# Block means of the first batch's values: ten products in one group of 32 array columns, or in four groups in turn with one product that adds them

## The chip, the cores and the metric

One NeuronCore of a Trainium2 chip. The time is device microseconds of one execution of the program. TensorE (PE) multiplies, VectorE (DVE), ScalarE (ACT) and GpSimd (POOL) do the element-wise work, SyncE (SP) requests the DMA transfers.

## What is computed

Two batches of windowed attention with block summaries, whose output goes through two feed-forward networks; the second network has the same shape, with another activation:

```python
B, H, S, D = 2, 8, 768, 64
block, window = (32, 16)
k_sum = k.reshape(B, H, nb, block, D).max(axis=3)
v_sum = v.reshape(B, H, nb, block, D).mean(axis=3)
# scores over a window of +-16 positions and over the 24 block maxima, one softmax over both
scores_all = np.concatenate([scores_l_m, scores_s], axis=-1)
v_all = np.concatenate([v, v_sum], axis=2)
x = np.matmul(a, v_all)                  # then 1536 tokens x 512
h = x @ w_in                             # 512 x 2048
out = activation(h) @ w_out              # 2048 x 512
```

The change is in `v_sum` of the first batch.

## The kernel before

Tokens are worked in 12 groups of 128 (six to a batch). A group g goes through `scores(g)` (PE products into two PSUM banks, then on DVE mask, scale and minimum, L520), `softmax(g)` (exponentials on ACT, L534, and the shares), `turn(g)` (transposes on PE, L574, and copies to SBUF), and `values(g)` (products on PE, L591, then a rounded copy, L601, and the rest, L603, into the two halves of the network's input). One chunk of the network is 512 tokens, so groups 0 to 3 must be through `values` before the first `first_product` (L637) can start. From there on products of the networks and the groups 4 to 11 alternate on PE.

Weights arrive as 64-bit numbers; `convert` and `split` (L298 to L327) turn each half of a weight tile into two single-precision parts by six passes on POOL, ACT and DVE.

`v_sums0` makes the 24 block means of the first batch. Six passes t run over the 768 positions. For t < 4 two products read the windowed values tiles (96 rows each, `blkw_sb`), for t = 4 and 5 one product reads 128 rows loaded for this alone (`v_a`, `blk_sb`). All ten accumulate in partitions 96 to 127 of one bank, `hs[3]`. The means are then copied to rows 96 to 119 of the six values tiles (L445 from PSUM for two of them, L449 from the first tile for the others), because `values` reads them as extra rows of its operand. `v_sums1` does the same for the second batch with 128-column products in four groups of the array's columns (L471).

Nothing is left to a scheduler. Every piece of work is an operation added with `Plan.add`, which takes the data it reads and writes and, where several engines could do it, their forms. `PICK` holds one digit for each such operation, the form taken. `ORDER` holds two characters for each operation, its number; the operations of each engine are issued in this order, and `Plan.idle` puts filler products of zeros (L1045) where it expects PE to wait. DMA requests all go through SP's queue in the same order. The tile framework adds the waits.

```python
                if t < 4:
                    for w in range(2):
                        mm(ps[96:P, :], blkw_sb[:, w, t, :], v[:96, w, :], start=(t + w == 0), stop=False)
                else:
                    mm(ps[96:P, :], blk_sb[:, t, :], v_a[:, t - 4, :], start=False, stop=(t == NG - 1))
```

Of the kernel before, what the change touches and what calls it, by code (L numbers as in the profile page):

```python
# [14 lines left out]
ALU = mybir.AluOpType  # L15
AX = mybir.AxisListType
# [5 lines left out]
NB = S // BLK  # L22
P = 128
# [28 lines left out]
    '0000230000000000001100111010000000011100001100000000000001000000110000000101110000001010000000000010'  # L52
    '0000000000000001000000000011020000002000001000100002001000200010000000000010000120010000001201001101'
    '0100100000110100010011010001001101011000201110001100101010111110000000101000001000001000000000000200'
    '1100000000011100000000100000010100002110001011001100001100010100000100110000010111100110100111000111'
    '1011000101000110100101010010100011011101010000111100010010110110011010111010101001010101011001011110'
    '1111110101011011000010111101100100010100011111000100110010001011000000110101011011100100111101001001'
    '01101000001111111000111101010011000101'
)
ORDER = (  # L60
    "###(#4#)#;#$#2#6#0#8#%%>#9#:#5#&%E#3#<#'#7#W#1%Z#V$&%?#?#B$(%@$7$'$.%A%F$8#=$)#@$9#A%L%H$Y%G$*$/%B$0"
    "$?%I#+$+$,&%$-$:$H$@$1$A&#$2%J$3$;&$$B%K$<$5$4$C&7$=%C$I#F#C$6$>%S$J$K#D&&#>$F#E$D&'$P%M#G$E%D$Z%N%#"
    "#H%$&0&)%O$L$Q&8$R%P#*#,$M&U&9#I&:%T'#%)$N%%&;#-%&%V$O&<#J$S%*%Q%'#K&=%+%U$T#.'H$G%($U#L#N$W$V#X#O%,"
    "#Z%W%.%-#P$#%2$X#Y#Q&3&Y&*#R%0&V&W%5&1%3&,#S%/%4%8%1'$%R%6%;%9%7%X#/'I':%<%:%Y(Y&+%=#T&2&-&>'J'K&4$%"
    "&.*X'L&5&/&?'M$$&@&D&(&Z&A&I'N&E&X+.+$&F(,&J&G&K&B'%&H*Y';&L&C')#M&M+%&N&6&P+/&O&Q+&*Z+2'<&R+0'.+#'*"
    "+<&S+3(-+''/(/+1(.&T#U+('B+4'&'++=+)'0+5',+*'-+J+@'1''+6'2'((H++'5+A+>'3+7'6+?+,'=+B(M(I+-,$+C'V'>+8"
    "'D+K(%+D+9'O'4+E+L'7+F+N+M(N+:+X+O'8(O,#+G(J+Q+;+Y'W,%'A+R+Z(P'Y,&'?'X,4'@'9'C+H(&,5(Z'Z,('P)#,2+I('"
    ")8'E(#(K+P(L(Q,3'G($'Q,E'F),(T(:,G(():(0(R(U+S,D(S'R,F)'+T(V'S+U(1,6()+V)()-,'(*).+W))(W'T(;)*)/,),X"
    "(2,:(X,Y(<(=)0)$,+,*)+(>'U,H)%,,)&,7(+(3)>,;,-,8(A)1)3(?,V)2)4(@,L,W,<)C)5)?,.,/,Z,9)6,I)@)D(6)E,0)7"
    ",J,=,M,K)A,>);,N)F,?,1,O-4)<)Q-#)O-&,@1Z)B)G)9)=(B-',P-1,A(C-2-(-5-$)J-8)P(D-3(4-%1L-0(5,Q)H,B-F-9)I"  # L70
    ',C)K-:-),R)Z(E(7-B-*,S)L-J-+-E,T*#-,-G-C,U)M(8-X-K)U-6)N--*$*%-7-D(9-Y)R.$)V-L)W1S-H-..%1M-;-U)X1O-I'
    "(F)S-W-<-T2%1N(G)T.6-M*&)Y2)-=*.-N*0-/*9-V->-O*'.1-?*(*).7-P...:-Q.0***:.&*/*;*4./-Z1P*+.8.;-R.H.#*<"
    ".<-@*,-A.'*-*5.22*1V*1.31T.(.4*6.L.Z*=*21U*3*G-S.).I*@*7.F/#.**8.5.X.+/&.E.9*L/'.D.M*>.J.W2#.=.V.K.>"
# [12 lines left out]
    "808S:%8V8R:18J918.;,8W928H848I8C:28L948X8K8E8M858D8Y868N958O96:'9)9+97939*9,8Z:-989/9-:P9#:390999.:Q"
    '9$;L:4;/:5;-9%9:;N9&9;9C9A:69<9@9E;2:7:&9B:.:9;M;P;0:(;&:W:/9F;1:)9D9=;3;R;.::9?;6;4;T9>;59G;O;79J;S'
    ";'9K;Q9I:;<#9H:X;Y;8;><$;9;E;U9N:8;V;:9O9V<%9L;;<&9M9Y>2;W9S;<9Z9P;=9T<;;Z9W;X>9</9X<69Q<5<'9R;?<=<<"
    '<(;@<)<A<><*:#<?>:>3<99U<B>4<4<@<+<C>5>;<0<,<8><<->6=B<1;F<J<E<2<D<.<V=C;A>7<W>=>8>@<F>>>?<:<G>A<H>B'
    ">C=T<I>D<K>E<L<N>V<M<R<3<O>F<7<S<P>G=U=D<Q?%<T=E<U;B=V?B=L=W;G=M<X?F>W?&;C?C;D?D?';H>H>X<Y;I>&=$?(=%"  # L90
    "?E<Z>Y;J=#;K?J?)=F>O>Z=)?#?*=(>'='=,=&?+?H?$=N>K=-?,=+=*?M?I?-?K?.=.>I?/?G=1>J?0=/?2=2?1?L=0B(?3=4B/"
    '=8=6?OB+B)?N=5?P=9B0=G===O>P@1B2=<@2?Q=:=@B*=3B,=7?R=;@3=?>(=>=X@7?U=Y=A@4@9>)@8@%@5@;B1?Y>LA8>QB3?V'
    "@:>R?ZA9B-@#@6B.@&>S=KB4B6=SB5=JB7=RB8=IB9B<B:@<=H@==PB;>M@>B=?SBL@'?T=Z@?>N>%>*@$?4=Q>.BS>$?W>#@@?X"
    '>T>-@AAKBMBO?5BN@(@B>U>1>+@L?;@H>,@M@D@,@C>/?7@)BT?6@IAJ@E?<BVBP>0@*BQ?8@.BU@F@+A:@0A;@/?9@-@G?:C8@N'
    'AB@O?=@RAC@J@SBW@K@PC9@QAL?>ATC:??BXA<?@C@?AA=C;BEB>BR@U@TAUBZCC@XBY@WBF@VC>@ZAMA$C#A#C<C$C(C)A&C?A*'
    "@YA(BHA'C%C=F%A+C&CGD'C'ADCHA%EVD(A)BAA,F&B?A-CACEEWD/CFEXAEA.EYCBA1A/A3D)D-D*EZA0F(D.A2D1E.AVA7BGAW"
    "CDANA5B@A6F'AABBCKD+A4CSAOBICOAICTA?CLCUA@D0CVAGF)AHAQA>AFBCCIF#BDE/BJBKF$C*D,C1CPAYF,F*D4CQCMCJARF+"
# [98 lines left out]
def tile_kernel(ctx, tc, qT, kT, kw, vw, vt, w1, w2, av, bv, masks, ident, blk, out):  # L199
# [220 lines left out]
    def v_sums0():  # L420
# [17 lines left out]
        for t in range(4, NG):  # L438
            load_v(t)
# [677 lines left out]
```

## Time and profile before

| | us |
|---|---|
| median of three runs | 589.99 |
| lowest and highest | 589.51, 591.37 |
| span of the profiled execution (first to last instruction) | 587.4 |
| PE busy in it | 578.6 |
| DVE, ACT, POOL busy | 494.4, 348.5, 294.7 |

The span is one execution under the profiler; the run's time is 2.6 us more at the median, which is what lies around the span. The granted clock of TensorE is 1.00 of full speed in every window of the profile. A product of single-precision operands stands in the trace as two records, each with its weight load. Times in the rows below are from the span's start.

### The profile page before, as it was taken

To read this page: it belongs to the slowest core of one execution; us is meant where nothing else is said; L and a number is where in the kernel's file an instruction comes from. 1 tells how busy PE (TensorE), PEld (TensorE's weight loads), DVE (VectorE), ACT (ScalarE), POOL (GpSimd) and SP (SyncE) were. 2 spreads that over 40 slices of the span, in tenths; PEclk is the share of its full clock that TensorE was granted. 3 is DMA by queue.
4 is the path that set the end of the run, shared out by engine and by line. 5 is a ranking of instruction groups with operands and counts; after the bars stand their busy time and mean duration, and the time that the engine had idled before them with its cause. 6 is when DMAs were issued, how large, how long until landed. Compare 5 with 4: busy or idle time off the path is not lost.

```text
span 587.4 us, 9645 instructions
## 1 busy us (share of the span) xinstructions
PE 578.6 (98%) x3608; PEld 466.6 (79%) x3613; DVE 494.4 (84%) x887; ACT 348.5 (59%) x648; POOL 294.7 (50%) x272
## 2 busy tenths in 40 slices
PE   8999999999999999999999999999999999999997
PEld 4477788888888888888888888888888888888886
DVE  5999999999989898988899998968687786866643
ACT  3988998988676677658657455524540434424410
POOL 1777676573475657654766472131423175523210
PEclk9999999999999999999999999999999999999999
DMA  8986534301222223110000141320313023002005
GB/s 311 352 306 209 192 118 151 104 30 35 73 71 73 76 101 110 37 36 2 17 20 1 37 143 37 107 73 0 144 32 113 1 73 126 18 0 73 1 1 214
DMA packets 17983, 53.10 MB, mean 90 GB/s; under 512 B 2273, under 2 KB 2785, under 8 KB 17937
## 3 DMA queue, kind: packets, MB, share of 16 engines
q1 hardware_dynamic: 17936, 52.49, 26.1%
q8 instruction: 28, 0.46, 0.3%
q14 instruction: 19, 0.15, 0.1%
HBM read 48.55 MB, written 3.15 MB: 88 GB/s over the span
## 4 chain that ended last, share of the span: by engine, by line
PE 94%; DMA 2%; DVE 1%; SPq 1%; issue 1%; POOL 0%; ACT 0%; DVEq 0%
PE y L654 23%; PE y L850 22%; PE hb L637 15%; PE hc L812 13%; PE hs L637 8%; PE hc L939 7%; PE hs L591 2%; PE hs L507 2%; PE hs L574 1%; DMA mask_sb<-in_masks 1%; DMA k<-in_blk 1%; SPq L280 1%; DVE s L520 0%; POOL s L549 0%; PE hs L434 0%
## 5 line engine op out<-in xcount | busy, mean ns | idle before, releaser
L654 PE MATMUL y<-g,wt 128*128 128x512 f32 x576 | 139.1, 392 | 0.0
L654 PEld LDWEIGHTS y<-g,wt 128*128 128x128 f32 x576 | 106.8, 188 | 22.3 <-POOL g L745 0.3
L850 PE MATMUL y<-wt,g 128*128 128x512 f32 x480 | 116.1, 389 | 0.0
L850 PEld LDWEIGHTS y<-wt,g 128*128 128x128 f32 x480 | 90.1, 188 | 18.7
L637 PE MATMUL hb<-xx,wt 128*128 128x512 f32 x384 | 89.5, 389 | 0.0
L325 POOL TENSOR_TENSOR wt<-raw,wt 128x512 fp32r<-128x512 f32 x44 | 62.4, 1425 | 51.0 <-DVE wt L322 30.4
L637 PEld LDWEIGHTS hb<-xx,wt 128*128 128x128 f32 x384 | 72.1, 188 | 15.0
L309 ACT ACTIVATE raw<-raw 128x512 f32<-128x512 f32 x62 | 41.1, 676 | 33.3 <-POOL raw L305 24.6
L717 POOL TENSOR_TENSOR q<-q,u 128x512 f32<-128x512 f32 x34 | 46.2, 1368 | 23.8 <-ACT u L707 14.4
L828 POOL TENSOR_TENSOR g<-t,g 128x512 fp32r<-128x512 f32 x17 | 23.4, 1380 | 63.3 <-ACT g L825 63.3
L825 ACT ACTIVATE g<-t 128x512 fp32r<-128x512 f32 x40 | 25.0, 628 | 49.4 <-PE y L850 43.4
L305 POOL TENSOR_SCALAR raw<-raw 128x512 f32<-128x512 f32 x44 | 35.8, 815 | 34.1 <-DMA raw<-in_w 33.9
L286 ACT ACTIVATE wt<-raw 128x512 fp32r<-128x512 f32 x56 | 36.8, 671 | 25.7 <-POOL raw L796 6.6
L313 DVE SCALAR_TENSOR_TENSOR raw<-raw 128x512 int32<-128x512 int32 x62 | 47.7, 779 | 4.3 <-ACT raw L309 4.1
L637 PE MATMUL hs<-xx,wt 128*128 128x512 f32 x192 | 47.8, 398 | 0.0
L812 PE MATMUL hc<-wt,wt 128*128 128x512 f32 x192 | 47.4, 389 | 0.0
L745 POOL TENSOR_TENSOR g<-t,g 128x512 fp32r<-128x512 f32 x22 | 30.6, 1397 | 30.3 <-ACT g L739 25.8
L939 PE MATMUL hc<-xx,wt 128*128 128x512 f32 x192 | 45.6, 389 | 0.0
L865 DVE SCALAR_TENSOR_TENSOR part<-y,part 128x512 f32<-128x512 f32 x36 | 24.4, 684 | 22.1 <-PE y L850 22.0
L939 PEld LDWEIGHTS hc<-xx,wt 128*128 128x128 f32 x192 | 36.0, 188 | 7.5
L812 PEld LDWEIGHTS hc<-wt,wt 128*128 128x128 f32 x192 | 36.0, 188 | 7.5
L637 PEld LDWEIGHTS hs<-xx,wt 128*128 128x128 f32 x192 | 35.1, 188 | 7.7 <-issue 0.2
(175 smaller groups left out, 1097.6 us busy)
## 6 DMA issues: line engine op xcount, KB each, us to landing
raw<-in_w SPq DMA_DIRECT2D x62, 512.0 KB, 4.2
vv<-in_vw SPq DMA_DIRECT2D x6, 512.0 KB, 7.1
out<-part SPq DMA_DIRECT2D x12, 256.0 KB, 2.9
k<-in_kT SPq DMA_DIRECT2D x4, 384.0 KB, 3.7
q<-in_qT SPq DMA_DIRECT2D x6, 256.0 KB, 7.5
e<-in_kT SPq DMA_DIRECT2D x4, 384.0 KB
raw<-in_vt SPq DMA_DIRECT2D x3, 512.0 KB, 5.1
e<-in_vw SPq DMA_DIRECT2D x3, 512.0 KB
```

What stands on the lines that cost most here:

```text
L286: nc.scalar.activation(out_, in_, AF.Copy)
L305: eng.tensor_scalar(out=hif, in0=hif, scalar1=CAP, scalar2=-CAP, op0=ALU.min, op1=ALU.max)
L309: add(ACT, 0.58, lambda: nc.scalar.activation(hif, hif, AF.Prelu, scale=REBIAS, alpha=2.0 ** 32), [kr], [(kr, 1)])
L313: add(DVE, 0.61, lambda: nc.vector.scalar_tensor_tensor(out=lo, in0=hi, scalar=3, in1=lo, op0=ALU.logical_shift_left, op1=ALU.bitwise_or), ...
L325: eng.tensor_tensor(out=to()[:, 1], in0=src, in1=to()[:, 0], op=ALU.subtract)
L637: mm(ps, lt, rt, start=(k == 0), stop=(k == 11))
L654: mm(y, lt, rt, start=(i == 0 and j == 0), stop=(i == HALF - 1 and j == 2))
L717: eng.tensor_tensor(out=q2[a][:, w], in0=q2[a][:, w], in1=u2[:, w], op=ALU.mult)
L745: eng.tensor_tensor(out=g2[a][:, 1, w], in0=t2[a][:, w], in1=g2[a][:, 0, w], op=ALU.subtract)
L812: mm(bank_at(bank_), left(lp, kk), right(rp, kk), start=(j == 0), stop=(j == 5))
L850: mm(yb[d], lt, rt, start=(j == 0 and e == 0), stop=(j == QUART - 1 and e == 2))
L939: mm(bank_at(2 * a + u), w_at(n)[:, lp, kk * P:(kk + 1) * P], x_of(2)[:, rp, kk, :], start=(j == 0), stop=(j == 11))
```

## The change

The ten products no longer all go to partitions 96 to 127. Product w of pass t < 4 goes to group c = (2t + w) mod 4 of 32 columns (partitions 32c to 32c + 31), passes 4 and 5 to groups 0 and 1; the first product in each group starts its sum, the last one ends it. Then the whole bank is copied to SBUF (`part`, on ACT or DVE by the form) and one product with `four_sb`, four 32x32 identities one below the other, adds the four groups into partitions 96 to 127, from where all goes on as before. `four_sb` is made on DVE from the identity matrix. The warm-up products become one operation instead of four. `PICK` and `ORDER` are new as a whole; the order of issue differs in all parts of the kernel.

```diff
+    four_sb = k_0[:, 3808:3840]
...
-        for n in range(4):
-            add(PE, 1.5, lambda: [mm(hs[2], z[:, :P], z, start=True, stop=True) for _ in range(4)],
-                ["z"], [("h", 2)])
+        add(PE, 6.0, lambda: [mm(hs[2], z[:, :P], z, start=True, stop=True) for _ in range(16)], ["z"], [("h", 2)])
...
+        add(DVE, 0.2, lambda: nc.vector.tensor_reduce(
+            out=four_sb, in_=id_sb.rearrange("p (x m) -> p m x", m=32), op=ALU.add, axis=AX.X), ["id"], ["four"])
...
-                if t < 4:
-                    for w in range(2):
-                        mm(ps[96:P, :], blkw_sb[:, w, t, :], v[:96, w, :], start=(t + w == 0), stop=False)
-                else:
-                    mm(ps[96:P, :], blk_sb[:, t, :], v_a[:, t - 4, :], start=False, stop=(t == NG - 1))
-
-            add(PE, 1.72 if t < 4 else 0.86, go, [("v", "b"), vk] if t < 4 else ["blk", ("v", "a", t - 4)], [("h", 3)],
+
+                parts = [(blkw_sb[:, w, t, :], v[:96, w, :]) for w in range(2)] if t < 4 else [(blk_sb[:, t, :], v_a[:, t - 4, :])]
+                for w, (mean, rows) in enumerate(parts):
+                    c = (2 * t + w) % 4 if t < 4 else t - 4
+                    mm(ps[32 * c:32 * c + 32, :], mean, rows, start=(t < 2), stop=(t >= 3))
+
+            add(PE, 0.9 if t < 5 else 0.5, go, [("v", "b"), vk] if t < 4 else ["blk", ("v", "a", t - 4)], [("h", 3)],
                 fresh=(("h", 3),) if t == 0 else ())
+        part, pk = vs, [("vs", c) for c in range(4)]
+        add(ACT, 0.5, lambda: nc.scalar.copy(part, ps), [("h", 3)], pk,
+            more=[(DVE, 0.6, lambda: nc.vector.tensor_copy(part, ps), False)])
+        add(PE, 0.9, lambda: mm(ps[96:P, :], four_sb, part, start=True, stop=True), ["four", *pk], [("h", 3)])
...
-            old = [("k", 0, p) for p in range(4)] + [("q", "b"), "blk"]
+            old = [("k", 0, p) for p in range(4)] + [("q", "b"), "blk", "four"]
```

How the new order of issue stands on PE until the first product, read from the two strings:

| before | after |
|---|---|
| scores 0, 1, 3, 2 | scores 0, 1, one turn of 0, scores 3, 2 |
| both turns of 0, means t = 0, both turns of 1 | means t = 0, a turn of 1, the other of 0, means t = 1, 2, the other turn of 1 |
| means t = 1, 2, 3, 4, 5 | means t = 3, 4, 5, the product with `four_sb` |
| turns of 2, a turn of 3, values 0, the other turn of 3 | turns of 2, values 0, a turn of 3, values 1, the other turn of 3 |
| values 1, 2, 3, scores 4, first product | values 2, 3, scores 4, first product |

The last diff line lets chunk 2 of the network's input, which takes over the tile in which `four_sb` stands, wait for its reader.

## Rows read from the trace of the kernel before

**Rows 1.** Page, part 1: busy us (share of the span) and instructions of each engine.

```profile
PE 578.6 (98%) x3608; PEld 466.6 (79%) x3613; DVE 494.4 (84%) x887; ACT 348.5 (59%) x648; POOL 294.7 (50%) x272
```

**Rows 2.** Windows: length, busy us (instructions) by engine, PEclk, DMA share, GB/s.

```profile
...
10.00:20.00 10.00, 8.40 (x229) 6.06 (x225) 9.26 (x55) 9.17 (x31) 6.29 (x10) 1.00 1.04 395
20.00:30.00 10.00, 9.68 (x31) 2.96 (x29) 9.57 (x39) 9.68 (x36) 7.49 (x14) 1.00 0.98 333
30.00:40.00 10.00, 8.68 (x212) 6.88 (x211) 9.87 (x18) 8.73 (x17) 7.46 (x8) 1.00 0.98 319
40.00:60.00 20.00, 19.58 (x277) 15.75 (x274) 18.53 (x72) 17.99 (x58) 16.53 (x18) 1.00 0.60 207
60.00:80.00 20.00, 19.91 (x211) 15.72 (x201) 19.55 (x51) 19.19 (x47) 12.42 (x14) 1.00 0.56 182
80.00:100.00 20.00, 20.00 (x239) 16.31 (x238) 18.99 (x58) 18.07 (x47) 15.34 (x15) 1.00 0.42 137
...
```

**Rows 3.** PE timeline: start, us, instruction, count, [idle before <-releaser].

```profile
19.22 1.90 PE L432 MATMUL hs<-vv,e 96*32 96x512 f32 x4 [0.24 <-DMA vv<-in_vw]
...
22.07 5.34 PE L432 MATMUL hs<-vv,e 96*32 96x512 f32 x12
...
27.73 1.88 PE L434 MATMUL hs<-v_a,k 128*32 128x512 f32 x4 [0.32 <-DMA k<-in_blk]
...
31.62 1.15 PE L591 MATMUL hs<-pt,vv 120*64 120x64 f32 x32
...
36.46 1.03 PE L1045 MATMUL hs<-z 128*128 128x512 bf16 x4 [0.16 <-issue]
...
38.72 0.40 PE L507 MATMUL hs<-k,q 64*64 64x96 f32 x8
...
39.97 3.01 PE L637 MATMUL hs<-xx,wt 128*128 128x512 f32 x12
```

**Rows 4.** DVE and ACT timelines, from the mask to the last values copies.

```profile
10.62 0.28 DVE L520 CUSTOM_DVE_ANT_0 s<-y,mask_sb 128x120 f32<-128x120 f32 x1 [1.51 <-DMA mask_sb<-in_masks]
...
36.71 1.27 DVE L603 TENSOR_TENSOR xx<-hs,xx 128x512 fp32r<-128x512 f32 x2
...
11.32 0.38 ACT L534 ACTIVATE s<-s,stat 128x120 f32<-128x120 f32 x1
...
36.61 0.57 ACT L601 CAST xx<-hs 128x512 fp32r<-128x512 f32 x1
```

**Rows 5.** Request queue's timeline, page part 6 (last: us to landing), chain of waits.

```profile
30.40 0.44 SPq L280 DMA_DIRECT2D q<-in_qT  x1
...
q<-in_qT SPq DMA_DIRECT2D x6, 256.0 KB, 7.5
...
21.45 6.15 DMA k<-in_blk
```

**Rows 6.** PE timeline: the second batch's block means, in four column groups.

```profile
58.72 1.52 PE L471 MATMUL hs<-raw,k 128*32 128x128 f32 x48 [0.24 <-ACT pt L577]
```

**Rows 7.** Groups by line and shape, 8 to 40 us: busy, mean ns.

```profile
L313 DVE SCALAR_TENSOR_TENSOR raw<-raw 128x512 int32<-128x512 int32 x7 | 4.6, 681 | 0.0
...
L325 DVE TENSOR_TENSOR wt<-raw,wt 128x512 fp32r<-128x512 f32 x2 | 1.9, 940 | 0.0
...
L376 DVE TENSOR_REDUCE ks<-e 128x24 f32<-128x768 f32 x2 | 1.9, 938 | 0.0
...
L578 DVE COPY t<-hs 120x512 f32<-120x512 f32 x2 | 1.4, 688 | 0.1
...
L305 DVE TENSOR_SCALAR raw<-raw 128x512 f32<-128x512 f32 x2 | 1.1, 530 | 0.0
...
L549 DVE TENSOR_TENSOR s<-s,stat 128x480 f32<-128x480 f32 x1 | 0.6, 645 | 0.0
...
L546 DVE TENSOR_SCALAR stat<-stat 128x4 f32<-128x4 f32 x1 | 0.2, 224 | 0.0
...
L577 ACT COPY pt<-hs 120x512 f32<-120x512 f32 x2 | 1.2, 576 | 0.1
```

More of the change, by code (lines that the diff above doesn't have):

```diff
@@ L64 @@
[L64 to L73, printed above, removed]
@@ new lines @@
+    "*X#T&5&?'#&@&6&D%W&I&A'N&E&Z(,&F'<+.%X&J&G&B&K'%&H+$&L&C*Y&M')&X%Y&N+%&P&O'$*Z';&Q':'.'*+&&R'+(-(Y',"
+    "&V#U'-+<&S'/'0+#+/+2'1&T+0(.(/'2+3+''&+4+(+1+@'(+=''+5'5'6+)'3+6'=(0'4+7(1+*+J(H'V(2'@'O+A)#(%(M+8)8"
+    "++'7+B+>+,'?+K+9,$'8(I+-+:'A(J+L'>'W(N'9'C'X(Z+?'E(O'Y,(+M+C+;+Z+D(P'Z,#(Q(K'G(#+X+N,5'F)9(L+Q+Y+O'P"
+    "),(R+E,2(&+P(T,%+F,4(U($,3+R)-(((:'Q,6+G):+S+H(S).+T)'+I(V+U'R+V,G(W)O+W,&,D(;)()/,),E))(X(<,',V,7,*"
+    "(',W(=,8,+)$(>,:'S,,,F)*(?)0,H()(@)%)+)&,9(*,;)1,I,-)3,X(+)2)4,=,Y,<,L)5,.(A1L)>'T,/)P,Z'U)6,J,M)C)7"
@@ new lines @@
+    ",K(3,N);,>)?,0)@,?-4,O)Q,1)A)D)=-#-&)<(B)B)E,@-0)F-'-8)G-3-5-((4)H,P(D-2)Z(6,Q-1,A)J)I-F-9-$(5,R)K-%"
+    "-:,B(C(7)U)L(E,S-X(8,C)M-6)V,T)N)W-G-7-J-E*#(9(F)X*$)R-K)Y-;*%-L-),U-B-<)S-C*&-=-D->.$*'(G-V-*2)-T*4"
+    "-+1S.61Z-,*0-Y--*.*(*5)T-H-.*6-/*9-U-I*)-?.0**.%-W-Z.:2**+-@.#*:.&.7...;*,1T-M.H*--A.<-N*/.'-O.(-P*1"
+    '.2-Q.I*;*7.L*<2#./*=*3.8.D*2-R*8.1*L.M*@.9.Z*M-S.N.=*G.3.)*>1O.>/4.*.4.?/#*H1V*A.@*?.A.5.V/&.+.F2$.J'
+    "/'.G/$*I*N/(.K*B.,*O*P/F1M*F/%*E*C*J.-.O*K*D.P2,/).E.Q.B*S.R1U.Y.C/*.X.S/G*Q/+1N/2.T/,.W*R*T/1/81P/3"
@@ new lines @@
+    "/5.U/J/0/-/6*U1W/7/9/B*V/./T*W/H/E/K/;/:/C/I1Q/X1R/M/L2I/<2%1X/=/N/Y//2+2&/>2'/O/?/Z2(/@/U1Y0&05/P2P"
+    "0*2W/Q0'0+062J0,/A2-0(/W0C2Q/D0)/V2Z/R2X0#0-/S0$2.0.2/0%0:0G0/3&090D08000>2K0E070H2Y0;2R0F010=0<2L02"
+    "3#0R0I0?030@0J0A2S0S040K2M3$0L2N3%0B0M0V1$2O3X0U1(0N0Y3J0W1%0O0T1)1'141*1&0Q1+0Z3'2T131,0P1-1.161=1#"
+    "4#1A181>1/172U1B1@0X3(20103)3K1C3Y1?3Z111D151;3*1E194$1:1F4%1<3+4&3L211G3,4U1H3M1I222V3.122:3Q4'3N2;"
+    '1K2>3O3-1J3P2?3R4G2@2<253;262=3?3/4(332A3@2937233T2B4H3A244V3<282C273S3>302D4)324I3=364W2E313B4X354J'
@@ new lines @@
+    "DZFFE$FNECDSFGDUG1FHDYEKG6FOFPDWF<FQE#F=F6G4FRFSE&G2E%E)EDG9EEG5E'G3E;E(E*G;ELF?G=EME,FTE4E-E6E+E7F7"
+    "G8GUG7FVE5FWGVGIE=F8GWG>G<G?FUEGGEG@G:E>GAEOGJE<GBGKE?F9EFF:F@EIGCGXFAFXEHENGDG'H#ERH(EQGYEUG(G*GFGM"
+    "G#GGH%GZH$ESH*H&H'I,H+FYH)FZH,G$G)GQH-GLEPH.H0I?H/ETG%I.GHH8H1I>H2H4H3G+G,GPG&GOG-I/GNGTGSI-H<I6H>I7"
+    'H@GRHDH?HBHCHHH=H5HAH9H6HJHNH:H7HFHRHOI@I0HVIAI8I1HMHSH;HQHWI9IHHLHZHPI#HTI*HXI(HUIII)I$I4IBHYICI5IJ'
+    "I=IKI2I&I:I'HEIDHII<HGILI3IPIFIQI;I+I%INHKIGITIOIUIEIVIMIWIRIS"
```

72 lines of the change are left out of this document (31 added, 41 removed).

## The prediction

> **What bounds the kernel now.** I read the busy shares first, then the windows by stage, then PE's timeline up to the first product, and last the timelines of DVE, ACT and the request queue for what PE waits on. The shares [rows 1] put PE at 98%, which would make every saved matmul a gain; they are an average over two stages. The windows [rows 2] part them. From 80 us on PE is busy 20.00 of 20 us: there only PE work counts. From 10 to 40 us it is not PE that is full: PE has 8.40, 9.68 and 8.68 of 10 us, DVE 9.26, 9.57 and 9.87, ACT 9.17, 9.68 and 8.73, and the DMA share is 1.04, 0.98 and 0.98 at 395, 333 and 319 GB/s. The stage ends where the first product starts, at 39.97 us [rows 3]; from there PE has an unbroken list, so a shift of that point moves the end by as much, and PE work saved ahead of it moves nothing by itself. What PE does there says the same: after the four values passes (31.62 us on) it runs filler products of zeros at 36.46 us, and the scores of group 4 start only at 38.72 [rows 3].
>
> What it waits for then: the scores of group 4 need the PSUM banks that the values of groups 2 and 3 used, whose last split (L603 on DVE) ends at 36.71 + 1.27 = 37.98 us [rows 4], and the queries of group 4, requested at 30.40 us; with the median of 7.5 us to landing these come at 37.9 [rows 5] or, as the start of 38.72 suggests, some 0.7 later. The split in turn ends a list that keeps DVE occupied from 10.62 us, when the mask lands [rows 4], for 27.36 us. ACT's list is as tight: exponentials from 11.32, last copy of values done at 36.61 + 0.57 = 37.18 us [rows 4]. So the start is bound by the mask's landing plus a full list of DVE and ACT.
>
> **The change part by part: the block means on PE.** Today eight products of 96 rows and two of 128, 512 columns each, go to the same 32 columns of the array. Each is two records, 20 in all, which take 1.90 + 5.34 + 1.88 = 9.12 us [rows 3]: 5.34/12 = 0.445 us a record, 0.89 a product. In the new code product w of pass t goes to column group (2t + w) mod 4. That groups run at once is shown by L471, which already deals its products to the four groups: 48 records of 128 columns in 1.52 us [rows 6], 32 ns each. At the rate above, a record of 128 columns would take 0.445/4 = 0.111 us alone, 5.3 us for 48: so about 3.5 at a time. The order strings can be read (two characters are one operation's number): in the new one PE has pass 0, two turns, passes 1 and 2, a turn, passes 3, 4 and 5, the new product. Two products side by side then cost about 0.89; passes 1 and 2 are on different groups and run as one; 3, 4 and 5 use four groups once. That is three times 0.89 plus overhangs, some 3 us, and the new product of 128 rows is half of the two at 1.88, 0.94 [rows 3]. PE work falls from 9.1 to about 4, by 5 us. By the argument above this lies ahead of 39.97 us in a stage that PE does not bound, so I cost it at nothing; were PE the bound it would be the whole gain (rival 1).
>
> [...]
>
> **The chain of the sums.** It grows by two links: after the last block-mean product, a copy of all 128 rows out of PSUM and the product with four identities, then the copies to the values tiles as before. The chosen form of the copy is ACT; the nearest row, a copy of 512 columns from PSUM, has 0.58 us, DVE's has 0.69 [rows 7]. With 0.94 for the product and about 0.2 us to hand over twice, the links add 1.9 us; the last two means now run side by side, which gives back 0.9. Against that the last input of the means is requested after 8.12 MB instead of 8.63 MB (the sizes of all requests ahead of it, added up in the order of the string): 0.51 MB at 333 GB/s [rows 2] is 1.5 us earlier. The chain of waits shows the DMA of blk, landing at 27.6 us, as what held these means [rows 5]; it now stands ahead by 0.77 MB. Sum: +1.0 - 1.5, the sums are ready 0.5 us earlier, or 0.5 later if ACT, on which the copy stands behind three exponential passes, is late. Four identities (a DVE reduction of 128 columns; the bounds are 0.22 and 0.65 us, as DVE's smallest row and a pass of 480 columns [rows 7]) stand ahead of the mask in DVE's list, where DVE idles 1.51 us for the mask today [rows 4]: nothing. If the cover goes, at most 0.65 us.
>
> **The order of DMA requests.** One half of the first weight moves up ahead of the first queries, and mask goes back: 2.85 MB are asked for up to and including it instead of 2.48. 0.37 MB at 395 GB/s [rows 2] is 0.93 us: the mask lands at about 11.5, and DVE's and ACT's lists start that much later. The queries of group 4 move up from 11.70 to 9.40 MB, 7 us at 319 to 333 GB/s, so the wait for them (37.98 to 38.72) disappears; the chain that is late next is the last split again.
>
> **DVE's list from the mask to the last split.** Read out of the two strings with their forms, it loses one L305, one L313, one L325, two L376 (keys of the second batch, pushed behind the first product) and one L549: 0.53 + 0.68 + 0.94 + 2 x 0.94 + 0.65 = 4.68 us [rows 7]. It gains five L546 at 0.22, one L578 at 0.69, one L601 and one L445 from PSUM, taken as L578, and one L449 of 24x1024, of which DVE has no row: between one L578 and two; I take 1.0. Together 1.1 + 3 x 0.69 + 1.0 = 4.2 us. Net -0.5. The last split then ends at 37.98 + 0.93 - 0.5 = 38.4. What is unsure here is DVE's own speed: L305 and L325 have means above what their size asks for when Pool works beside them (L305 0.53 on average over two [rows 7]), and the order mixes the two anew. Some 20 such passes by 0.05 us either way is +-1 us.
>
> **ACT's list** between the first exponential and the last copy of values loses five passes of 512 columns (two weight copies, a sums copy, a turn copy, a values copy) and gains one weight pass, the new copy, a share of four pieces of 0.38 [rows 4] and a constant of 0.2: -3 x 0.58 + 1.5 + 0.2 = 0.0. Its end moves from 37.18 to 38.1, the split behind it takes 0.64 [rows 4] and 0.2 to hand over: 38.9. The later of the two lists counts: scores of group 4 between 38.5 and 39.0 instead of 38.72, first product -0.2 to +0.3. I take +0.2.
>
> **Behind the first product** the PE work is the same in both; what can move are its waits. They are small: 0.42 us of idle in 40 to 60, 0.09 in 60 to 80, none after [rows 2]. More weight passes are already done at that point in the new order, and the second batch's keys and block means are pushed together behind it. I cost the two at nothing, with a bound of 0.5 us below and 1.5 above (three loads of 0.5 MB, which wait in turn for freed buffers, ahead of the second batch's means, which PE now reaches about 3 us sooner in its list).
>
> **The sum.** The profiled span of 587.4 lies 2.6 below the median of 589.99. 587.4 + 0.2 + 2.6 = 590.2 us.
>
> **The rivals.** 1: PE is the bound of the start after all, and its 5 us come through: the turns of groups 1 to 3 wait for PE, and with PE free the values start earlier. For it: PE is busy 9.68 of 10 in 20 to 30. Against it: DVE and ACT are as full there, and the means waited for DMA [rows 5]. In full 585, half of it 587.6. 2: DVE's list runs shorter than I add up, since Pool disturbs it less and more weight passes are done in the idle time ahead of the mask: 1 to 2 us, 588 to 589. 3, the slower side: the sums' chain sets the values. If the last input of the means lands no earlier than today (28 us), the new copy starts behind ACT's exponentials and the product ends at about 31 instead of 29.6; each group's values pass, split and the first product follow, and the first product is 1.5 to 2 us later: 591.5 to 592.2. It decides from a landing later than about 27 us. 4: the second batch's means stall PE in 50 to 60 us for their loads, up to 1.5 us: 591.7. 5: the groups do not run at once for 96-row products: PE work grows by 0.94, and with a start that PE doesn't bound that is 590 to 591.
>
> **How the numbers follow.** A measurement of this kernel can tell 0.3%, 1.8 us, from no change. Forecast (first product within 1.5 us of today's, no new stall) 0.56; rival 1 0.12; rival 2 0.12; rival 3 0.10; rival 4 0.08; rival 5 0.02. The forecast's own range, from +-1 us of DVE's speed and the two ends of ACT's and DVE's lists, is 588.6 to 591.6. Taking in rival 2, half of rival 1 and most of 3 and 4 gives 587.4 to 592.2. Faster (below 588.2): rival 1, half of rival 2 and a little of the forecast, 0.20. Slower (above 591.8): half of 3 and 4 and the forecast's edge, 0.17. Same: 0.63.
>
> **What would show it.** In the profile after: the means' records overlapping, with less than 5 us on PE; the first DVE mask pass at 11.3 to 11.8; the last split of group 3 at 38 to 39 and no wait behind it for queries; more filler or idle time on PE between 20 and 38 us, of about the 5 us that were saved; the first product at 39.7 to 40.5; windows full from 80 us on. The prediction is wrong if the first product starts before 38.5 (rivals 1 and 2), if it starts after 41.5 (rival 3), or if PE idles over 1 us between 45 and 65.

## The result and the profile after

The changed kernel takes 593.91 us (median of 5 runs, 592.89 to 595.23); the kernel before takes 590.49 beside it. The ratio of the times is 1.006, with a 95% interval of 1.0043 to 1.0077: 3.5 us slower, outside the range forecast. Ratios further down are to runs of the kernel before taken beside each, with the same kind of interval in brackets. The profiled run has a span of 591.3 us, 3.9 more than that of before, and 593.05 us as its own time.

TensorE's share is as high as in [rows 1], and its busy time has grown by 2.4 us, although the means need less of it (page, part 1: busy us, share, instructions):

```profile
PE 581.0 (98%) x3640; PEld 467.2 (79%) x3640; DVE 489.0 (83%) x908; ACT 350.9 (59%) x650; POOL 272.4 (46%) x254
```

The windows, in the columns of [rows 2], with one late stretch added:

```profile
core 0: us, PE busy (x) PEld busy (x) DVE busy (x) ACT busy (x) POOL busy (x), PEclk, DMA share, GB/s
10.00:20.00 10.00, 8.97 (x214) 5.95 (x218) 8.64 (x47) 8.54 (x33) 5.12 (x6) 1.00 0.93 330
20.00:30.00 10.00, 8.14 (x112) 3.37 (x104) 8.97 (x48) 8.44 (x30) 7.94 (x8) 1.00 0.96 346
30.00:40.00 10.00, 9.68 (x156) 6.71 (x156) 8.77 (x19) 9.28 (x19) 6.03 (x12) 1.00 1.02 378
40.00:60.00 20.00, 19.65 (x335) 15.04 (x333) 19.01 (x74) 19.14 (x56) 12.32 (x14) 1.00 0.62 217
...
450.00:460.00 10.00, 9.05 (x39) 6.83 (x38) 6.91 (x12) 2.41 (x4) 3.66 (x4) 1.00 0.17 52
```

The same late stretch of the kernel before:

```profile
450.00:460.00 10.00, 10.00 (x46) 8.29 (x45) 5.06 (x9) 0.68 (x1) 1.93 (x3) 1.00 0.22 81
```

Three things stand out. In 10 to 40 us VectorE is busy 26.38 us, where it was 28.70 before: the list that was full has holes. The DMA share of 10 to 20 us has fallen from 1.04 to 0.93. And at 450 to 460, where TensorE had no idle time, it now has 0.95 us.

TensorE's timeline up to the first product, in the columns of [rows 3]:

```profile
22.18 1.05 PE L435 MATMUL hs<-vv,e 96*32 96x512 f32 x4 [0.83 <-DMA vv<-in_vw]
...
24.19 1.05 PE L435 MATMUL hs<-vv,e 96*32 96x512 f32 x4
26.27 1.05 PE L435 MATMUL hs<-vv,e 96*32 96x512 f32 x4 [1.03 <-DMA vv<-in_vw]
...
27.83 1.05 PE L435 MATMUL hs<-vv,e 96*32 96x512 f32 x4
28.51 1.62 PE L435 MATMUL hs<-v_a,k 128*32 128x512 f32 x4
30.06 1.04 PE L1050 MATMUL hs<-z 128*128 128x512 bf16 x4
31.02 1.05 PE L442 MATMUL hs<-e,k 128*32 128x512 f32 x2
...
33.55 1.03 PE L596 MATMUL hs<-pt,vv 120*64 120x64 f32 x28 [0.20 <-ACT vv L450]
...
40.68 0.40 PE L512 MATMUL hs<-k,q 64*64 64x96 f32 x8
...
41.94 1.42 PE L642 MATMUL hs<-xx,wt 128*128 128x512 f32 x5
```

The first product starts at 41.94 rather than 39.97 [rows 3], 1.97 us later; the values at 33.0 rather than 31.62, the product with the four identities ends at 32.07. What released each step is in the chain of waits (start us, us, what):

```profile
6.09 7.04 DMA raw<-in_w
...
13.21 0.66 POOL raw L306
13.87 1.27 POOL wt L326
15.16 0.33 SPq L299
...
17.20 9.02 DMA vv<-in_vw
...
26.27 1.05 PE hs L435 x4
```

Read it backwards. The means of the third value tile wait for its landing at 26.22 us. Its request went out at 17.20, behind others on the request queue, the first of which, the second half of weight 3, went out at 15.16; the request before that was at 10.81, so for 4.35 us the queue asked for nothing. It waited for the buffer that this half goes into, and that was freed by a Pool pass (L326, the low half of the second part of weight 0). That pass stood in Pool's list behind a clamp (L306) of the first part, which waited for its own landing at 13.13. In [rows 2] 10 to 20 us has 395 GB/s; here it is 330.

The kernel before has such a wait on its request queue too, 5.49 us from the request at 13.36 to the next:

```profile
18.85 0.33 SPq L298 DMA_DIRECT2D raw<-in_w  x1
```

But there three of the four value tiles are asked for ahead of it, in the new order none.

VectorE's first mask pass, its last split, and ScalarE's new copy and last values copy, beside [rows 4]:

```profile
12.04 0.28 DVE L525 CUSTOM_DVE_ANT_0 s<-y,mask_sb 128x120 f32<-128x120 f32 x1
...
39.33 1.30 DVE L608 TENSOR_TENSOR xx<-hs,xx 128x512 fp32r<-128x512 f32 x2
...
30.16 0.59 ACT L440 COPY e<-hs 128x512 f32<-128x512 f32 x1 [1.45 <-PE hs L435]
...
39.34 0.57 ACT L606 CAST xx<-hs 128x512 fp32r<-128x512 f32 x1
```

The scores of group 4 start at 40.68, right behind that split's end (40.63): no query is waited for. And the late idle time, on four engines at 452 to 457 us:

```profile
452.06 0.85 POOL L801 TENSOR_TENSOR raw<-raw 128x256 f32<-128x256 f32 x1 [5.89 <-DVE raw L801]
...
453.87 0.70 ACT L287 ACTIVATE wt<-raw 128x512 fp32r<-128x512 f32 x1 [5.97 <-POOL raw L801]
...
453.87 0.89 DVE L801 TENSOR_TENSOR raw<-raw,raw 128x256 f32<-128x256 f32 x1 [1.30 <-POOL raw L801]
...
454.44 0.71 ACT L827 ACTIVATE t<-hc,lnb 128x512 f32<-128x512 f32 x1
...
455.88 0.67 DVE L828 SCALAR_TENSOR_TENSOR t<-t,hc 128x512 f32<-128x512 f32 x1
...
456.61 1.67 PE L817 MATMUL hc<-wt,wt 128*128 128x512 f32 x6 [0.95 <-DVE t L828]
```

A weight step on ScalarE (L287) waits 5.97 us for Pool. The activation step L827, which needs nothing of it, stands behind it in ScalarE's list and starts only at 454.44. L828, the next step on VectorE, stands there behind a weight step (L801) that waits 1.30 us for Pool, and behind two more passes; the product waits for L828. From the product (L817) at 445.70 to this one at 456.61 TensorE takes 10.91 us; in the three kernels below that issue the same products without this wait it takes 9.52. So the place costs 1.4 us, of the 1.9 that the span loses behind the first product.

### The profile page after: what moved, and what is told of

It is laid out like the page before. It is cut to its first block, busy times and chain, and to the rows that moved or that the text cites. A ratio compares the mean times of both kernels' runs of the same rounds, so it can differ in the third digit from the quotient of the medians.

```text
span 591.3 us, 9716 instructions
## 1 busy us (share of the span) xinstructions
PE 581.0 (98%) x3640; PEld 467.2 (79%) x3640; DVE 489.0 (83%) x908; ACT 350.9 (59%) x650; POOL 272.4 (46%) x254
## 4 chain that ended last, share of the span: by engine, by line
PE 87%; DVE 4%; DMA 4%; SPq 1%; POOL 1%; issue 1%; ACT 1%; DVEq 0%; POOLq 0%; ACTq 0%
PE y L659 22%; PE y L855 19%; PE hb L642 15%; PE hc L817 12%; PE hs L642 8%; PE hc L944 6%; DMA raw<-in_w 3%; PE hs L512 2%; DMA vv<-in_vw 2%; PE hs L596 1%; PE hs L579 1%; SPq L281 1%; DVE t L828 1%; DVE wt L326 1%; PE hs L435 1%
## 5 line engine op out<-in xcount | busy, mean ns | idle before, releaser
L326 POOL TENSOR_TENSOR wt<-raw,wt 128x512 fp32r<-128x512 f32 x35 | 49.6, 1421 | 57.6 <-ACT wt L287 26.6
L833 POOL TENSOR_TENSOR g<-t,g 128x512 fp32r<-128x512 f32 x21 | 27.8, 1333 | 67.0 <-ACT g L830 45.9
L306 POOL TENSOR_SCALAR raw<-raw 128x512 f32<-128x512 f32 x43 | 34.7, 814 | 39.0 <-DMA raw<-in_w 38.3
L817 PE MATMUL hc<-wt,wt 128*128 128x512 f32 x192 | 47.7, 390 | 1.0 <-DVE t L828 1.0
L287 ACT ACTIVATE wt<-raw 128x512 fp32r<-128x512 f32 x44 | 29.0, 671 | 23.9 <-POOL raw L801 16.4
L817 PEld LDWEIGHTS hc<-wt,wt 128*128 128x128 f32 x192 | 36.0, 188 | 8.8 <-DVE t L828 1.4
L326 DVE TENSOR_TENSOR wt<-raw,wt 128x512 fp32r<-128x512 f32 x43 | 31.1, 732 | 11.1 <-ACT wt L287 10.5
```

Source lines behind the costliest of these rows:

```text
L287: nc.scalar.activation(out_, in_, AF.Copy)
L306: eng.tensor_scalar(out=hif, in0=hif, scalar1=CAP, scalar2=-CAP, op0=ALU.min, op1=ALU.max)
L326: eng.tensor_tensor(out=to()[:, 1], in0=src, in1=to()[:, 0], op=ALU.subtract)
L817: mm(bank_at(bank_), left(lp, kk), right(rp, kk), start=(j == 0), stop=(j == 5))
L833: eng.tensor_tensor(out=g[:, 1], in0=t, in1=g[:, 0], op=ALU.subtract)
```

## The experiments

The theory after the result: the order of issue, not the new means, costs the time, in two places, the request queue at the start and ScalarE's and VectorE's lists at 455 us. The rival: the means themselves, by their two added links.

**The two halves of the change.** One kernel has the new means in the old order, the other the old means in the new order.

```
means_alone:  old ORDER and PICK; four_sb ahead of pass 1, part copy and four-identity product behind pass 5
order_alone:  old v_sums0; ORDER and PICK of the changed kernel, without its three new operations
```

> The kernel before with its own order and forms; only the block means are the new ones (four column groups, the copy on ACT right behind the last of them, the product with the four identities behind it, the identities made on DVE just before pass 1). Theory A (the loss is the new order of issue): within 1 us of before, 589.5 to 591.5, first product at 39.6 to 40.6 us, PE not waiting in the second network. Theory B (the two added links in the sums' chain cost what was lost): first product near 42 us, 592.5 to 594.

> The kernel before, block means in one group as before, with the new order of issue and the new forms. Theory A: as slow as the changed kernel, 593 to 594.5: the request of the half weight again waits until about 15 us with the value tiles behind it, the first product starts at 41.2 to 42.2, and PE waits again some 1.5 us in the second network. Theory B: the first product back at 40 us, 591.5 to 592.5 (the wait in the second network stays).

The old means in the new order take 593.31 us (5 runs), ratio 1.0053 [1.0033, 1.0073], as slow as the whole change, with the first product at

```profile
42.36 1.89 PE L637 MATMUL hs<-xx,wt 128*128 128x512 f32 x7
```

The wait that both theories expected at 455 us was not in that trace. The chain for it is there, with a weight step on ScalarE that waits 5.99 us for Pool, but it ends 0.7 us earlier (453.18, not 453.87), and TensorE comes to the product 0.6 us later (456.23, not 455.66) and finds its input ready. So the late wait does not follow from the order alone. The new means in the old order take 591.27 (12 runs, 588.54 to 595.82), ratio 1.0020 [0.9998, 1.0041]: inside Theory A's time, but scattered over 7 us, and the profiled run, one of its two longest, has its first product at 45.98, later than either theory. So the order carries the loss; whether the means add to it in the old order is taken up below.

**The request queue.** Three edits of the changed kernel's start. One gives the second half of weight 3 a buffer that is free, so that its request waits for nothing.

```
+            if ph == 0 and i == 3 and k == 1:
+                seq[0] += 1
+                raw = e0[:, 1024:2048].bitcast(I32)
+                special = 6, raw.rearrange("p (n two) -> p n two", two=2), [("v", "c")]
```

> The changed kernel with one edit: the second half of weight 3 is loaded into memory that nothing uses then, so its request does not wait for the buffer of weight 0 (the next half that used this buffer no longer waits for weight 3 either). Theory A1 (the wait in the request queue, with four value tiles behind it, makes the sums late): the value tiles are asked for from about 12 us on instead of 16.1, the block means end some 2 us earlier, the first product starts at 39.9 to 40.6 instead of 41.9, and the time falls by 1.3 to 2 us to about 592. Theory B (the added links): the means end as late as before or the first product moves by less than 0.5 us, 593.5 to 594.

Its requests, and its first product:

```profile
11.21 0.43 SPq L299 DMA_DIRECT2D e<-in_w  x1
...
12.27 3.04 SPq L281 DMA_DIRECT2D vv<-in_vw  x4
```

```profile
40.52 1.65 PE L646 MATMUL hs<-xx,wt 128*128 128x512 f32 x6
```

The value tiles are asked for 3.8 us earlier, the first product comes 1.42 us earlier, and the time is 592.18 (11 runs), ratio 1.0034 [1.0017, 1.0051], as Theory A1 has it. The interval overlaps that of the changed kernel. The profiled run, at 593.67 us the longest of the eleven, does not keep the gain: by the product at 457.21 (456.61 in the changed kernel) it is lost again, in part to new waits of 0.25, 0.29 and 0.42 us at 199, 349 and 453 us. The late wait is still in its trace.

The second leaves the buffers alone and moves the waiting request behind the value tiles.

```
 request queue:  t(weight 2)
-                raw(weight 3, 2nd half: waits for a buffer)
                 blk, value tiles 0 to 3
+                raw(weight 3, 2nd half)
                 blk (keys' place), last two value tiles
```

> The changed kernel; on the request queue one entry is moved, weight 3's second half, which waits for a buffer until 15.2 us, from ahead of the block table and the four value tiles to right behind them. Theory A (what delays the first product is that the value tiles stand behind a request that waits): the value tiles are asked for from about 11.9 us rather than 16.1, the last means pair runs near 26 rather than 27.8, the first product comes at 39.9 to 40.8 rather than 41.9, time 592.0 to 593.0 (593.9 less 1.0 to 1.9). Theory B (the delay is the weight's own lateness, or the new means' chain): weight 3 now comes no earlier, or later, and the first product stays at 41.7 to 42.5, time 593.5 to 594.5.

Neither came: 596.69 us, ratio 1.0124 [1.011, 1.0137]. The value tiles are asked for from 11.4 us, as Theory A wanted, but the half of weight 3 then lands at 25.0, and VectorE's list has it in front of what the values need:

```profile
25.04 0.43 DVE L312 TENSOR_SCALAR raw<-raw 128x512 int32<-128x512 int32 x1 [5.35 <-DMA raw<-in_w]
```

VectorE stands still for 5.35 us, and the first product comes at 46.33. The queue of requests and the lists of the engines fit each other in this order; one of them cannot be turned alone.

The third brings forward what the request waits for, by exchanging two neighbours in Pool's list.

```
 Pool:  clamp (weight 0, part 2)
+       low half (weight 0, part 2)      # frees the buffer
        clamp (weight 0, part 1)         # waits for its landing
-       low half (weight 0, part 2)
```

> The changed kernel with two neighbours in Pool's list exchanged: the low half of weight 0's second part, which frees the buffer, is issued ahead of the clamp of its first part, which waits for a landing until 13.2 us. No buffer and no transfer is added, and the order of the requests is the changed kernel's. Theory A (the request queue waits for this one Pool pass, and the four value tiles and weight 3's half stand behind it): the pass runs at 12.9 to 14.2 rather than 13.8 to 15.1, the waiting request goes out near 14.2 rather than 15.16, first product 41.0 to 41.5 rather than 41.9, time 593.0 to 593.5. Theory B (the clamp that now comes 0.9 later delays as much, or the values wait for another thing): first product at 41.8 to 42.5, time 593.8 to 594.5.

```profile
12.82 1.31 POOL L326 TENSOR_TENSOR wt<-raw,wt 128x512 fp32r<-128x512 f32 x1 [2.23 <-ACT wt L287]
```

```profile
14.16 0.33 SPq L299 DMA_DIRECT2D raw<-in_w  x1
```

```profile
40.84 3.02 PE L642 MATMUL hs<-xx,wt 128*128 128x512 f32 x12
```

One Pool pass 1.02 us earlier, the request 1.00 earlier, the first product 1.10 earlier; no transfer and no buffer changed. The time is 592.58 (6 runs), ratio 1.0051 [1.0034, 1.0067], below Theory A's 593.0 to 593.5. The interval overlaps that of the changed kernel, so the gain in time is not shown by the runs alone; the trace shows the place.

**The late wait.** First all of the second network's operations were put back to their old places and forms.

```
 operations of the first network:   ORDER and PICK of the changed kernel
-operations of the second network:  ORDER and PICK of the changed kernel
+operations of the second network:  ORDER and PICK of the kernel before
```

> The changed kernel, but all operations of the second network stand at the places in the order, and in the forms, that they had before. Theory A: the start stays (first product at 41.9), the wait of PE for a DVE product at 455 us goes, and the time falls by 1.3 to 1.7 us to about 592.3. If the late wait only follows from the late start, or moves to another place: unchanged, 593.9.

Neither came: 606.0 us, ratio 1.0277 [1.0252, 1.0302]. Between 300 and 375 us the trace has a wait of 4.0 us of TensorE for VectorE (L750), and more of that kind: two orders spliced make waits that neither has. It says nothing of the wait at 455. Then only the two activation steps were moved.

```
 ScalarE:  + L827 (activation)      VectorE:  + L828 (activation)
             L287 (weight)                      L801 (weight)
           - L827                             - L828
```

> The changed kernel with two operations of the second network issued earlier on their own engines: the two activation steps (ScalarE's and VectorE's, some 0.5 us each) that make the input of the product at 456 us go ahead of the two weight steps that wait for the third of three loads. The start is untouched: first product at 41.9. Theory A (those two steps are held behind the weight steps in their queues, and that is the 1.5 us lost between 450 and 460): the wait of the product there goes, the lag of TensorE's work against before stays at +2.1 to +2.6 past 460, time 592.2 to 592.9. Theory B (the load that lands late is needed by the products right behind anyway): the wait only moves behind 460, lag +3.5 to +3.9, time 593.5 to 594.2.

```profile
453.29 0.68 DVE L828 SCALAR_TENSOR_TENSOR t<-t,hc 128x512 f32<-128x512 f32 x1
```

```profile
456.32 1.52 PE L817 MATMUL hc<-wt,wt 128*128 128x512 f32 x6
```

L828 runs 2.6 us earlier and the product has no idle time in front of it; from the product before (at 446.28) it is 10.04 us rather than 10.91. But this trace came to 446 us 0.58 us later than that of the changed kernel, so the product starts only 0.29 earlier. 592.82 us (5 runs), ratio 1.0051 [1.0038, 1.0064]: inside Theory A's time, but the interval overlaps that of the changed kernel, and the gain in time is again not shown by the runs alone.

**Both together**, with the free buffer and with the exchange in Pool's list:

```
free_late_swap = free_buffer + late_swap
pool_late      = pool_swap + late_swap
```

> The changed kernel with both: weight 3's second half loaded into a free buffer (first product then at 40.5, as that edit alone gave), and the two activation steps of the second network moved ahead of the weight steps. Theory A (the loss of 3.9 us is two separate waits, one of the order of requests at the start, one of the order of two queues at 455): the gains add, 592.2 less 1.0 to 1.5, 590.7 to 591.2. Theory B (the late wait follows from when the third load lands, whatever is issued ahead of it): 592.0 to 592.6.

> The changed kernel with both exchanges, of the two Pool passes at the start and of the two activation steps at 455 us: four operations moved, nothing else. Theory A: the two gains add, 592.8 less 0.5 to 0.9, 591.9 to 592.4. Theory B (the exchange at the start gives nothing): 592.6 to 593.2.

The free buffer with the late exchange takes 591.08 us (8 runs), ratio 1.0024 [1.0014, 1.0034], below the interval of the changed kernel and inside what Theory A expected. It is the one kernel here whose gain the runs alone show. By the ratios the single edits give back 1.5 and 0.5 us and both 2.1, so the two losses look separate. Its first product is at 40.09. The four operations moved in the other take 591.53 (8 runs), 1.0032 [1.0016, 1.0047], faster than Theory A's 591.9 to 592.4, by less than the runs scatter; its trace, of a run of 592.54, has the request at 14.39 but the first product only at 42.23, for a reason that comes below. Together the edits take back 2.1 of 3.5 us of the ratio with the buffer and 1.7 without.

**The scatter of the new means in the old order.** The profiled run of that kernel is one of its long ones. TensorE has few fillers ahead of the fourth value tile; it is busy 0.84 of 3 us in 23 to 26, and then its granted clock is 0.50 of full speed and the two products that read that tile take 1.92 us, where the changed kernel has 1.05:

```profile
26.00:29.00 3.00, 3.00 (x8) 0.43 (x4) 1.81 (x6) 1.93 (x5) 1.25 (x4) 0.50 0.96 318
29.00:32.00 3.00, 3.00 (x8) 0.32 (x6) 2.00 (x3) 0.53 (x2) 2.70 (x4) 0.51 0.99 371
```

Nine fillers were added there.

```
-                for _ in range(times):
+                for _ in range(times + 9 * (i == 36)):
```

> The new means in the old order, with nine more products of zeros (0.25 us each) in the gap of 2.2 us that TensorE has ahead of the means of the fourth value tile, so that it does not idle there. Theory A (the saved TensorE work is not free: in that gap the granted clock falls, the profile of the kernel without the products shows 0.50 in 26 to 32 us, records of the means at 1.92 rather than 1.05 us, and runs spread over 7 us): granted clock 1.00 from 23 to 32 us, the product with the identities at 30.2 to 31.2 rather than 32.2, first product 39.6 to 40.6, time 589.5 to 590.6 with little spread. Theory B (the fall of the clock lies beside other waits, or the spread has another cause): time 590.8 to 591.8, with the same spread.

The clock stays at 1.00 from 20 to 40 us and the product with the identities comes at 30.70 rather than 32.16, but the time is Theory B's, 591.11 (12 runs, 589.11 to 593.2), ratio 1.0024 [1.001, 1.0038]. So the clock was not what the median lost. But it goes with the longest runs: without the fillers the two runs above 593 us (594.66 and 595.82) are the two whose mean granted clock is 0.99, and the nine at 0.999 or 1.00 have a median of 590.90. Both traces have a stop of TensorE inside the last values, with nothing waited for that the profile shows:

```profile
41.57 0.45 PE L596 MATMUL hs<-q,vv 120*64 120x64 f32 x7 [1.85 <-issue]
```

```profile
39.88 0.69 PE L596 MATMUL hs<-q,vv 120*64 120x64 f32 x16 [1.91 <-issue]
```

The first trace stops with 7 records of the values left, the second, with nine more products in front, with 16 left: nine more. The kernel before has such a stop too, among its fillers, where it is not seen in [rows 3] as more than a gap (rows of the weight loads):

```profile
36.23 0.76 PEld L1045 LDWEIGHTS <-z 128*128 128x128 bf16 x5
38.40 0.10 PEld L1045 LDWEIGHTS <-z 128*128 128x128 bf16 x1 [1.40 <-issue]
```

So the theory, inferred from these three stops: TensorE runs out of instructions at a fixed count. Three kernels move that count.

```
before_plus12:  warm-up of 28 products of zeros (12 of 512, 16 of 128 columns) in place of 16 of 512
means_warm8, before_warm8:  warm-up of 4 fp32 products (8 weight loads) in place of 16 bfloat16 ones (16)
means_warm8_free:  means_warm8 + the free buffer of above
```

> The kernel before, with twelve more and as many narrower products of zeros in the warm-up (28 rather than 16, of the same 8192 columns in sum), and nothing else. In three traces of the old order TensorE stands still after its 487th weight load and goes on 2 us after an instruction packet has started: 36.9 to 38.4 among products of zeros in the kernel before, 39.5 to 41.6 and 37.8 to 39.9 among the values where the means are new. Theory A (TensorE runs out of instructions at a fixed count, and the new means move that count from the zeros into the values): twelve loads more put the 487th some 7 values from their end, TensorE stands still there for 1.2 to 2.1 us, first product 40.5 to 42.0, time 590.0 to 591.5, with a wider spread. Theory B (the pause hangs on time or on the new means, not on the count): the pause stays among the zeros at 36.5 to 38.5, first product within 0.4 of 39.97, time 589.0 to 590.2.

> The new means in the old order, with the warm-up of sixteen bfloat16 products of zeros (16 weight loads) made of four fp32 products of as many passes (8 weight loads). Theory A (the pause after the 487th weight load is what the new means cost in the old order): eight loads fewer put it behind the last of the values, among the zeros, as in the kernel before; first product 39.6 to 40.6, time 589.3 to 590.4, less spread than the 588.5 to 595.8 without the edit. Theory B (the cost is the low granted clock of the means, 0.50 in 26 to 32 us, or the chain of the means): 590.8 to 591.8, the same spread.

> The kernel before, with the same warm-up of eight weight loads fewer: the 487th falls behind the zeros, into the scores that stand ahead of the first product. Theory A: the first scores run ahead of the pause and the rest behind it; the pause ends when the instruction packet has come, not later than before, so the first product stays within 0.5 of 39.97 or comes up to 0.6 earlier: 588.8 to 590.0. Theory B (the warm-up itself matters, by the clock or by the first scores): the first scores at 8 us come later by over 0.5 us, 590.0 to 591.0.

> The new means in the old order with the warm-up of eight loads fewer, and weight 3's second half loaded into the free buffer, so that the fourth value tile is asked for near 14 rather than 19.2 us. Theory A (behind the means the start is bound by the mask and by the lists of VectorE and ScalarE): the means end 1 to 3 us earlier and the first product does not move by over 0.5 us against the run without the buffer: 589.0 to 590.4. Theory B (the fourth value tile is what the start waits for): first product 1 to 2 us earlier than without, 587.8 to 589.0, and faster than both kernels.

(The 487 of these texts takes in the waits of TensorE's queue; 474 or 475 of them are weight loads.) Where there is a stop, it is at this count (474 in before and before_plus12, 475 in means_alone, means_filled and means_warm8). The kernel before with twelve more products stops inside the values, with 7 left:

```profile
38.22 0.31 PEld L591 LDWEIGHTS hs<-q,vv 120*64 120x64 f32 x7 [2.04 <-issue]
```

The windows from the start to the end of the stop have the same number of weight loads (second pair) in the kernel before and, below it, in this one:

```profile
0.00:38.38 38.38, 33.69 (x470) 18.37 (x474) 31.14 (x112) 27.95 (x81) 21.94 (x37) 1.00 0.95 335
```

```profile
0.00:38.20 38.20, 32.50 (x474) 18.50 (x474) 30.11 (x110) 26.08 (x77) 20.57 (x37) 1.00 0.95 336
```

With eight fewer, the new means have the stop among the fillers again:

```profile
37.60 0.11 PEld L1052 LDWEIGHTS <-z 128*128 128x128 bf16 x2
38.71 0.53 PEld L1052 LDWEIGHTS <-z 128*128 128x128 bf16 x3 [1.00 <-issue]
```

With as many fewer in the old means' kernel (before_warm8) there is no stop at that count.

What a stop costs can be seen in two places. The exchange in Pool's list alone (pool_swap) and the same with the late exchange (pool_late) issue the same work up to 446 us, and at the last values pass their traces are 0.21 us apart (36.92 and 37.13). The first has no stop and its first product at 40.84; the second stops for 1.00 us among the values and has its first product at 42.23. And behind the three stops of about 2 us among the values the granted clock falls, to 0.52 in means_filled and before_plus12:

```profile
41.00:44.50 3.50, 3.50 (x68) 2.38 (x66) 2.83 (x5) 3.50 (x8) 0.88 (x1) 0.52 0.89 339
```

```profile
39.00:42.50 3.50, 3.50 (x57) 2.10 (x59) 2.83 (x5) 3.50 (x8) 0.78 (x1) 0.52 0.87 316
```

In means_alone, the third, the scores behind the stop take as long as in these two, 0.60 and 0.37 us for eight records each, where the kernel before has 0.40 and 0.26. The first products of the three come at 44.53, 42.85 and 45.98. Behind the shorter stops the clock is 1.00, in 40 to 45 us of means_warm8 and means_warm8_free and in 40 to 60 us of the kernel before [rows 2]; in pool_late the scores take 0.40 and 0.26 us.

Over all runs it costs less. The profiled run of before_plus12 has a span of 589.8, 2.4 above that of before, but over 12 runs this kernel takes 590.93 us, ratio 1.0012 [0.9994, 1.0029]: its four runs at a mean clock of 0.996 or 0.997 have a median of 592.66, its eight at 0.999 or 1.00 one of 590.35. means_warm8: 591.62, 1.0013 [0.9997, 1.003], first product at 40.91, which is Theory B's time. before_warm8: 590.52, 1.000 [0.998, 1.002], again Theory B's, although its profiled run has the first product at 39.17, 0.8 earlier than [rows 3]. means_warm8_free: 592.16, 1.0033 [1.0015, 1.0052], above both theories, first product at 40.73, so the earlier fourth tile gave nothing. Where the stop falls is shown; that it is what lowers the clock in the long runs is only argued, since each kernel has one trace. Nor is the clock all of the scatter: the kernel before takes 588.83 to 592.97 us in the 35 runs beside these, the longest of them at a clock of 1.00.

Nothing that ran is faster than the kernel before.

## Why the prediction was wrong

**The bound** was named rightly: the first product's shift of 1.97 us is half of the span's 3.9, and saving TensorE's work ahead of it gave nothing. Its time of the means was mis-sized: 1.05 three times, 2.30 for the last three passes and 1.05 for the product are 6.5 us, not 4, against 9.12. Passes 1 and 2, taken to run side by side, are apart, since the tile of pass 2 lands 2.8 us after that of pass 1 (26.22 and 23.39). Two products in two groups take 1.05 us, not 0.89, where two in one group take 1.90 [rows 3]. None of this reached the end: the same order with the old means is as slow. What the trace shows ahead of these products is the landing of their operands: TensorE waits 0.83 us for it in pass 0 and 1.03 us in pass 2.

**The chain of the sums is the step that failed**, in one term. The two links were put at 1.9 us and took 1.94 (30.13, the end of the means, to 32.07). But the last input was to land 1.5 us earlier, because 0.51 MB less stands ahead of it. It is the 128 rows of pass 5 (`v_a`), and the product that reads them waited for their landing and started 0.85 us later than before. First the changed kernel, then the kernel before:

```profile
29.08 0.14 PEld L435 LDWEIGHTS hs<-v_a,k 128*32 128x32 f32 x2 [0.46 <-DMA v_a<-in_vt]
```

```profile
28.23 0.11 PEld L434 LDWEIGHTS hs<-v_a,k 128*32 128x32 f32 x1 [0.39 <-DMA v_a<-in_vt]
```

With the last two means side by side, the means were to end 2.4 us earlier and ended 0.5 later (30.13 against 27.73 + 1.88 [rows 3]). Bytes over a rate tell when a transfer lands only while the rate holds, and it fell: 330 rather than 395 GB/s from 10 to 20 us is 0.65 MB less, more than the 0.51 MB saved. The new order has a request that waits 4.35 us for a buffer, and the four value tiles and these rows stand behind it. The order string showed that request's place and the buffer it needs; I counted its bytes and did not ask what it waits for.

**The rival that came** is the third: it was to decide from a last landing later than about 27 us. The fourth value tile landed at 27.47 and the rows of pass 5 at 29.0, the product ended at 32.07 (31 was said), the first product came 1.97 later (1.5 to 2 was said). In one point it came otherwise: the copy did not stand behind exponentials, ScalarE waited 1.45 us for the means. It had a chance of 0.10. Its price alone, 591.5 to 592.2, ends below the measured time because a second loss, behind the first product, came on top.

**The mask** was first used at 12.04 rather than 11.5 (the bytes asked for 0.93 us, measured 1.42). **The lists** of VectorE and ScalarE were added up as if they stayed full; the last split was to end at 38.4 to 38.9 and ended at 40.63, since VectorE idled 2.3 us more in 10 to 40. A sum over a list bounds it from below once its inputs come late. **The queries** of group 4 came in time, as said. The four identities took 0.41 us ahead of the mask, inside the bounds.

**Behind the first product** the bound of 1.5 us was the right size in the wrong place. It named the second batch's means, 50 to 60 us, where 0.14 us is waited for; 1.4 us of the loss stand at 456 us. "None after 80 us" was read off the old order, but the order and the forms are new in all parts of the kernel, so every stage's waits had to be asked for anew.

**What stays open.** With both waits taken away 0.24% is left, 1.4 us. In that trace the first product is 0.12 us later than in [rows 3], and TensorE has new idle time of 0.24 us in 150 to 200 and 0.31 in 300 to 350; the rest of the 2.0 us between the two spans has no place. What the new means cost in the old order the runs tell only roughly: the three kernels that have them without the free buffer are at 1.0013 to 1.0024, and of these one interval, that of means_filled, lies clear of 1. Why the late wait is in the changed kernel and not in order_alone, beyond the 0.6 to 0.7 us between them, is open too.

## What to carry to other kernels

Before a landing is worked out from bytes, ask of each request ahead of it what it waits for: here one buffer still in use held the request queue for 4.35 us with the four value tiles behind it, and the pass that frees the buffer stood behind a clamp that waited for an unrelated landing until 13.13 us. When an order of issue is new as a whole, price it as a whole: a list of the waits of the old order says nothing of the new one. Two neighbours exchanged in one engine's list can show such a chain without touching buffers or transfers; putting the blocked request behind the others did not cure it but made it worse (596.69 us).

## What the runs showed of the hardware

In 7 of the 16 traces TensorE stops, with nothing waited for that the profile shows, whatever work stands there. Between weight loads it is 1.40 us in the kernel before, 2.04 in before_plus12, 1.93 in means_alone and 1.00 in means_warm8; between products it is 1.91 us in means_filled, 0.80 in means_warm8_free and 1.00 in pool_late. In five of them 474 or 475 weight loads stand ahead of it. In means_warm8_free it comes behind the same product of zeros as in means_warm8, and in pool_late behind the 14th record of the last values, where the changed kernel has its 473rd load. So the old order stops in six kernels of seven, the new one in one of nine.

Each of the two kernels compared has 28 packets of the kind "instruction" on one DMA queue, 0.46 MB in all. In the kernel before the third starts at 35.97 us, 0.93 us ahead of the 474th weight load (36.90), and TensorE goes on at 38.40, 2.43 us after the packet's start. In the changed kernel the third starts at 32.9, 5.5 us ahead of the 474th load (38.40), and there is no stop. In means_filled such a packet starts between 37.6 and 38.0, and TensorE goes on at 39.88. The traces do not name the engine that the packets are for; that they are TensorE's, and that the stop is a wait for one of them, is inferred from these times. pool_swap and pool_late show both kinds, without a stop and with one of 1.00 us, in the same work. Why the packet comes later in the kernel before than in the changed one, with the DMA share at 0.95 up to the end of the stop, was not tried.
